# SyncE's first 40 transfers, each held until the third last has landed, in an attention and two-MoE kernel

## The chip, the cores and the metric

The kernel runs on one core of one Trainium2 chip. The metric is the time of one execution in microseconds of the device. Three runs of the kernel before gave a median of 592.82 us (592.39 to 595.15).

## What is computed

A gated linear attention with a state is followed by two expert-free feed-forward layers, all in 32-bit floats. The reference, cut to what matters:

```python
# attention: x [4, 8, 768, 32], a [4, 8, 768], B and C [4, 8, 768, 16], in chunks of 32
log_a = np.log(np.clip(a, 1e-06, 1.0))
for c in range(nc):
    L = np.exp(cum[:, :, :, None] - cum[:, :, None, :]) * causal      # cum: running sum of log_a
    y = (einsum('bhin,bhjn->bhij', C, B) * L) @ x                     # inside the chunk
    y += einsum('bhin,bhnd->bhid', C, state) * np.exp(cum)[..., None] # from the chunks before
    state = decay_full * state + sum_j(B_j x_j * decay_from_j)
# layer 1, tokens 3072 x 256:   h = x @ w_in (256 x 2048); x = (h * sigmoid(h)) @ w_out (2048 x 256)
# layer 2:                      h = x @ w_in
#   x = ((a0 + a1 h + a2 h^2 + a3 h^3) / (1 + |b0| |h| + |b1| h^2 + 1e-6)) @ w_out
```

## The kernel before

The 3072 tokens are 24 tiles of 128 tokens, tile `n` holding 128 positions of one of the 4 batches. For each of them one `tok` tile of 128 x 768 floats (384 KB: x, B and C in two layouts) is loaded (`attention`, line 668), into a ring of six. A visit of TensorE (`visit`, line 851) then makes that tile's attention, in one PSUM tile `att`, and the result is written as `y1h` and `y1l`, a rounded part and the rest, which the matmuls use in place of one 32-bit operand. Before a visit, VectorE or GpSimd multiply parts of the tile by decay factors: `Ea` at lines 720 and 724, `eL` at line 713. For the first three tiles the factors in `Ea` are computed in place. For all others they are computed once in two pieces, stored to the DRAM tensor `dre` (line 576) and loaded again, each row 16 times, by seven `Ea` loads (line 688, `E_LOADS`).

Layer 1 (`layer1_block`, line 954) goes through the tokens in six blocks of 512, and in each through 16 pieces of the hidden width: six matmuls of 128 x 512 into `h`, Silu, a split into two parts, six matmuls into `acc`. Its weights come in 16 raw tiles of 512 KB (`weights`, line 584, load in line 590, a ring of three `wraw` tiles), as 64-bit words that ScalarE, VectorE and GpSimd turn into two 32-bit parts `w` (lines 603 to 631). The weights of layer 2 take the same way, go out to DRAM as `w2s` and come back when layer 1 is done with its own. Layer 2 (`layer2_block`, line 1008) does the same with a rational function in place of Silu, and stores six output blocks.

All 113 transfers are issued by one engine, SyncE, in one order, and it stops at the first whose wait is not over. Which order this is, on SyncE and on every other engine, is decided when the program is built: each piece of work has a key (the table `K`, lines 34 and following), and a planner (`Plan.run`, line 243) starts, engine by engine, the ready piece with the smallest key, with its own costs per piece. The semaphores that the instructions wait for are then derived from the tiles that they share. Eight of them, DMAHW0 to DMAHW7, are used for transfers in turn; so a transfer already waits for the one eight places ahead of it.

The first transfers in order: `la` (the gates), `cum` and `con` (constants), four `tok` tiles, three `wraw` tiles, `abt` (the six coefficients), the two stores to `dre`, two `tok` tiles, and then `Ea` loads, `tok` tiles and `wraw` tiles mixed. Until the attention has begun, TensorE also runs 23 matmuls on zeros (line 530).

Of the kernel before, what the change touches and what calls it, by code (L numbers as in the profile page):

```python
# [7 lines left out]
F32 = mybir.dt.float32  # L8
# [6 lines left out]
P = 128  # L15
B, H, S, D, N = 4, 8, 768, 32, 16
# [8 lines left out]
WC = 2 * DM  # L25
# [4 lines left out]
NB2 = 512  # L30
HALVED = 0
HEAD = 0
TAIL_FLEX = 1
K = dict(
    half0=193.588,
# [150 lines left out]
R6 = NSUB + NCH  # L186
# [41 lines left out]
class Plan:  # L228
# [9 lines left out]
    def add(self, choices, key, deps=(), new=(), use=(), wr=(), rd=(), cols=0, after=0.0, big=True, soft=False):  # L238
        op = Op(choices, key, list(deps), list(new), list(use), wr, rd, cols, after, big, soft)
        self.ops.append(op)  # L240
        return op
# [94 lines left out]
def ssd_moe_moe_kernel(ctx: ExitStack, tc: tile.TileContext, tok, la_in, consts, w1, w2, ab, outT):  # L336
# [17 lines left out]
    def ring(tag, n, cols, dt=F32, space="SB", pad=0):  # L354
        rings[tag] = (Ring(n), n, cols, space, pad)

    counter = [0]

    def new(tag, dt=F32, cols=None):
        r, n, width, space, pad = rings[tag]  # L360
# [29 lines left out]
    def load_table(set_id):  # L390
        ACT.add_instruction(
            mybir.InstLoadActFuncSet(
                name=nc.get_next_instruction_name(),
                act_func_set_id=set_id,
                engine=mybir.EngineType.Activation,
                ins=[],
                outs=[],
            )
        )
# [60 lines left out]


    cum = new("cum")
    ld_la = add({"SP": (0.1, lambda: (load_table(SET_LN_EXP), nc.sync.dma_start(la, la_in)))}, 0.0)

    def f_cum():
        cum.t = cum.make()
        nc.sync.dma_start(cum.t[:, 0 : C_CEND - C_CUM], consts[:, C_CUM:C_CEND])

    ld_cum = dma(0.1, 197e3, f_cum, new=[cum])
    ld_con = dma(0.2, 101e3, lambda: nc.sync.dma_start(con, consts[:, 0:C_CUM]))  # L470
    ld_ab = dma(25.0, 3e3, lambda: nc.sync.dma_start(abt, ab))

    def f_ab():
        ACT.activation(absb, abt[:, 4:6], AF.Abs)
# [96 lines left out]
    for i, first in enumerate((0, NTB - P // H)):  # L571
        Ee, a = factors(lambda first=first: la[:, first * H : first * H + P], K["bulk"] + 2 * i, [], None)

        def f_dre(i=i, Ee=Ee, skip=0 if i == 0 else 2 * P // H - NTB):
            ns = slice(i * P // H, min(NTB, (i + 1) * P // H))
            nc.sync.dma_start(dre.rearrange("h n e -> n h e")[ns], Ee.t[skip * H :, 0 : P + R6])

        o_dre.append(dma(K["bulk"] + 2 * i, 68e3, f_dre, [a], use=[Ee]))
    decays(4, NTB, K["late"], [])
# [4 lines left out]
    def weights(layer, f, k_load, key):  # L584
        src = (w1, w2)[layer][f]
        raw = new("wraw", U64 if wide else F32)

        def f_load():
            raw.t = raw.make()
            nc.sync.dma_start(raw.t if wide else raw.t[:, 0:WC], src)  # L590

        o = dma(k_load, P * WC * (8 if wide else 4), f_load, new=[raw])
        val, value = raw, lambda: raw.t[:, 0:WC]
        if wide:
            v = new("wv")

            def words():
                w = raw.t.bitcast(U32).rearrange("p (n w) -> p n w", w=2)
                return w[:, :, 0], w[:, :, 1]

            def f_exp():
                v.t = v.make()
                ACT.activation(v.t, words()[1].bitcast(F32), AF.Prelu, scale=2.0**-112, alpha=2.0**32)  # L603

            def f_bits(part):
                low = words()[0]
                vb = v.t.bitcast(U32)
                if part == 0:
                    DVE.tensor_scalar(vb, vb, 3, None, op0=ALU.logical_shift_left)  # L609
                else:  # L610
                    DVE.scalar_tensor_tensor(vb, low, 29, vb, op0=ALU.logical_shift_right, op1=ALU.bitwise_or)  # L611

            o = add({"ACT": (c_act(WC) + 0.025, f_exp)}, key, [o], new=[v], use=[raw])
            for part in range(2):
                o = add({"DVE": (c_dve(WC, part == 0), lambda part=part: f_bits(part), True)}, key + 0.1, [o], use=[raw, v])
            val, value = v, lambda: v.t

        part = raw if layer else new(f"w{f}")

        def halves():  # L620
            t = part.t.bitcast(F32R)
            return t[:, WC : 2 * WC], t[:, 0:WC]

        def f_hi():
            if not layer:
                part.t = part.make()
            ACT.activation(halves()[0], value(), AF.Copy)

        def f_lo(eng):
            hi, lo = halves()  # L630
            eng.tensor_tensor(lo, value(), hi, op=ALU.subtract)  # L631

        a = add({"ACT": (c_act(WC), f_hi)}, key + 0.2, [o], new=[] if layer else [part], use=[val, part])
        o = add(
            {"POOL": (c_ptt(WC), lambda: f_lo(POOL), True), "DVE": (c_dve(WC), lambda: f_lo(DVE), True)},
            key + 0.3, [a], use=[val, part],
        )
        if layer:
            dr = new("w2s")

            def f_out():
                dr.t = dr.make()
                nc.sync.dma_start(dr.t, part.t.bitcast(F32))

            return dr, dma(key + 0.4, P * WC * 8, f_out, [o], new=[dr], use=[part])
        w_at[f], o_w[f] = part, o

    def reload(f, key, dr, after):
        part = new(f"w{f}")

        def f_in():
            part.t = part.make()
            nc.sync.dma_start(part.t, dr.t)

        w_at[f], o_w[f] = part, dma(key, P * WC * 8, f_in, [after], new=[part], use=[dr])

# [11 lines left out]
    def attention(n, T, d, k_load):  # L668
        b, c = blk_of[n], n % TPB
        o = n * P  # L670
        t = new("tok")

        def f_load():
            t.t = t.make()
            nc.sync.dma_start(t.t[:, 0:TOK], tok[n])  # L675

        ld = dma(k_load, P * TOK * 4, f_load, new=[t])
        x = lambda: t.t[:, 0:DM]
        bw = lambda: t.t[:, DM : DM + P]
        bt = lambda: t.t[:, DM + P : DM + 2 * P]  # L680
        cx = lambda: t.t[:, DM + 2 * P : TOK]
        cs = lambda: t.t[:, TOK : TOK + DM]

        for n0, n1 in E_LOADS:
            if n == n0:

                def f_er(n0=n0, n1=n1):
                    nc.sync.dma_start(Ev[:, n0:n1, :], dre[:, n0:n1, :].unsqueeze(1).broadcast_to([H, N, n1 - n0, P + R6]))

                first, end = n0 * H // P, (n1 - 1) * H // P  # L690
                o = dma(k_load, 155e3 * (n1 - n0), f_er, o_dre[first : end + 1])
                o_ee.update(dict.fromkeys(range(n0, n1), o))
        e0 = lambda: Ev[:, n, P : P + R6]

        Gm = new("Gm")

        def f_gm(eng):
            Gm.t = Gm.make()
            eng.tensor_tensor(
                Gm.t.rearrange("p (h a i) -> p h a i", h=H, a=SPC),  # L700
                eG[:, :, n * H : (n + 1) * H].rearrange("p a h -> p h a").unsqueeze(3).broadcast_to([P, H, SPC, SUB]),
                tri.rearrange("p (a i) -> p a i", a=SPC).unsqueeze(1).broadcast_to([P, H, SPC, SUB]),
                op=ALU.mult,
            )

        by = {"POOL": (1.06, lambda: f_gm(POOL), True), "DVE": (c_dve(H * CH), lambda: f_gm(DVE), True)}
        if n < GM_POOL:
            del by["DVE"]
        o_gm = add(by, T, [o_eG[n], ld_con], new=[Gm])

        def f_bw():
            v = bw().rearrange("p (h n) -> p h n", h=H)
            POOL.tensor_tensor(v, v, eL[:, n, :].unsqueeze(2).broadcast_to([P, H, N]), op=ALU.mult)

        o_bw = add({"POOL": (0.4, f_bw, True)}, T + 0.5 * d, [ld, o_eL[n]], use=[t])


        def f_ce(eng):
            v = cx().rearrange("p (a i) -> p a i", a=2)
            eng.tensor_tensor(v, v, Ev[:, n, 0:P].unsqueeze(1).broadcast_to([P, 2, P]), op=ALU.mult)  # L720

        def f_cs(eng):
            v, o = (z.rearrange("p (a s i) -> p a s i", a=2, s=NSUB) for z in (cx(), cs()))
            eng.tensor_tensor(
                o, v, e0()[:, 0:NSUB].unsqueeze(1).unsqueeze(3).broadcast_to([P, 2, NSUB, SUB]), op=ALU.mult
            )

        o_ce = add({"POOL": (0.8, lambda: f_ce(POOL), True), "DVE": (c_dve(DM), lambda: f_ce(DVE), True)}, T + 0.5 * d, [ld, o_ee[n]], use=[t])
        o_cs = add({"POOL": (0.58, lambda: f_cs(POOL), True), "DVE": (c_dve(DM), lambda: f_cs(DVE), True)}, T + 2 * d, [o_ce], use=[t])

        at[n] = (t, T, d, ld, o_bw, [o_ce], o_cs, o_gm, Gm, x, bw, cs, bt, cx, e0)
# [276 lines left out]
    def layer2_block(b, t0, step, rh, rc, held_h, o_tab):  # L1008
# [85 lines left out]
        for d in range(2):  # L1094
# [7 lines left out]
                    DVE.tensor_copy(ov()[:, d, :], acc_t[d])  # L1102

            def f_store(d=d):
                nc.sync.dma_start(outT[:, d, lo_t:hi_t], ov()[:, d, :])

            choices = {"ACT": (c_act(NB2, True), lambda f_o=f_o: f_o(ACT)), "DVE": (c_dve(NB2), lambda f_o=f_o: f_o(DVE))}
            if final:
# [163 lines left out]
```

## Time and profile before

| | before |
|---|---|
| median of three runs | 592.82 us (592.39 to 595.15) |
| the profiled execution | 591.67 us |
| its span, first to last instruction | 589.8 us |
| TensorE busy | 577.5 us, 98% |
| VectorE, ScalarE, GpSimd busy | 434.7, 405.7, 301.5 us |
| mean granted TensorE clock | 0.994 |
| moved by DMA | 48.84 MB |

The span is what the profile covers; the 1.9 us around it belong to the execution but show no instruction. Busy shares are means over stages that differ: attention with layer 1 up to about 150 us, layer 1 alone, then layer 2 from about 300 us. An idle time of an engine is listed with what ended it (the releaser). A transfer's time to landing runs from its issue on SyncE to the last of its semaphore's counts.

### The profile page before, as it was taken

What the parts mean: (1) busy time and instruction counts of PE and PEld (TensorE: products, weight loads), DVE (VectorE), ACT (ScalarE), POOL (GpSimd) and SP (SyncE); (2) the same over time, 40 slices, a digit from 0 to 9 for tenths busy, and PEclk for the clock granted to TensorE, in tenths of its full rate; (3) what the DMA queues carried; (4) which work ended last, traced back from release to release, by engine and by line L of the source; (5) the groups of instructions that cost most, each with busy time, mean ns of one, the idle gap of its engine ahead of it and who ended that gap; (6) DMA issues with size and microseconds to landing.
All of it is one profiled execution on the core that took longest, in us unless ns stands there. A gap on an engine that the chain in (4) does not pass through costs nothing.

```text
span 589.8 us, 11914 instructions
## 1 busy us (share of the span) xinstructions
PE 577.5 (98%) x4589; PEld 463.8 (79%) x4589; DVE 434.7 (74%) x722; ACT 405.7 (69%) x728; POOL 301.5 (51%) x328
## 2 busy tenths in 40 slices
PE   7799999999999999999999999999999999999997
PEld 4477777777888888888888888888888888888885
DVE  4899999888522222222124999999999999999995
ACT  4466666456433544444446899989999999999994
POOL 4354416541112100100102788888888888888883
PEclk9799999999999999999999999999999999999999
DMA  7876566876300000000047500000000000000000
GB/s 249 260 238 229 199 198 241 293 234 221 144 1 0 1 0 1 1 1 0 1 138 230 203 1 1 37 1 1 36 1 2 37 1 0 36 2 2 36 2 36
DMA packets 16200, 48.84 MB, mean 83 GB/s; under 512 B 1872, under 2 KB 2960, under 8 KB 16144
## 3 DMA queue, kind: packets, MB, share of 16 engines
q1 hardware_dynamic: 16144, 48.09, 24.0%
q8 instruction: 36, 0.59, 0.4%
q14 instruction: 20, 0.16, 0.1%
HBM read 36.44 MB, written 11.64 MB: 82 GB/s over the span
## 4 chain that ended last, share of the span: by engine, by line
PE 87%; DVE 6%; DMA 3%; ACT 2%; SPq 1%; issue 1%; DVEq 0%; ACTq 0%
PE acc L402 42%; PE h L402 34%; PE b L402 8%; PE att L402 3%; DMA wraw<-in_w_dram 2%; DVE wv L611 1%; DVE w L631 1%; DVE wv L609 1%; DMA Ea<-dre 1%; DVE M L768 1%; ACT wv L603 1%; SPq L675 0%; DVE y1l L896 0%; ACT T L976 0%; DVE S L789 0%
## 5 line engine op out<-in xcount | busy, mean ns | idle before, releaser
L402 PE MATMUL h<-y1h,w 128*128 128x512 f32 x636 | 216.9, 391 | 0.4 <-ACT y1h L893 0.3
L402 PE MATMUL acc<-gh,w 128*128 128x512 f32 x768 | 207.1, 391 | 0.0
L402 PEld LDWEIGHTS acc<-gh,w 128*128 128x128 f32 x768 | 143.1, 188 | 30.6 <-ACT wraw L1100 0.3
L941 DVE TENSOR_TENSOR gl<-T,gh 128x512 fp32r<-128x512 f32 x85 | 59.7, 705 | 115.6 <-ACT gh L935 90.4
L402 PEld LDWEIGHTS h<-y1h,w 128*128 128x128 f32 x636 | 119.3, 188 | 26.9 <-ACT y1h L893 0.8
L941 POOL TENSOR_TENSOR gl<-g,gh 128x512 fp32r<-128x512 f32 x95 | 122.8, 1295 | 19.4 <-ACT gh L935 16.5
L402 PE MATMUL h<-y1l,w 128*128 128x512 f32 x318 | 123.9, 390 | 0.3 <-DVE y1l L896 0.3
L402 PE MATMUL acc<-gl,w 128*128 128x512 f32 x384 | 118.5, 389 | 0.0
L976 ACT ACTIVATE T<-h 128x512 f32<-128x512 f32 x96 | 57.1, 596 | 80.6 <-PE h L402 78.3
L937 POOL TENSOR_SCALAR gh<-T 128x512 fp32r<-128x512 f32 x21 | 14.1, 670 | 167.0 <-PE acc L402 122.9
L402 PEld LDWEIGHTS acc<-gl,w 128*128 128x128 f32 x384 | 72.1, 188 | 15.2
L1042 POOL TENSOR_SCALAR tok<-T,abt 128x512 f32<-128x512 f32 x96 | 74.3, 774 | 9.3 <-ACT T L1034 8.7
L1045 DVE SCALAR_TENSOR_TENSOR b<-T,absb,b 128x512 f32<-128x512 f32 x96 | 71.6, 751 | 2.6 <-ACT T L1034 1.7
L1063 DVE SCALAR_TENSOR_TENSOR g<-tok,abt,b 128x512 f32<-128x512 f32 x96 | 71.2, 743 | 0.9 <-ACT b L1057 0.3
L1054 ACT ACTIVATE b<-b,lnb 128x512 f32<-128x512 f32 x96 | 64.5, 673 | 8.4 <-DVE b L1045 8.0
L402 PEld LDWEIGHTS h<-y1l,w 128*128 128x128 f32 x318 | 59.7, 188 | 12.7 <-DVE y1l L896 0.6
L935 ACT ACTIVATE gh<-T 128x512 fp32r<-128x512 f32 x75 | 47.4, 632 | 26.1 <-PE acc L402 25.4
L1057 ACT ACTIVATE b<-b 128x512 f32<-128x512 f32 x96 | 57.4, 599 | 0.5
L1051 DVE SCALAR_TENSOR_TENSOR tok<-T,abt,h 128x512 f32<-128x512 f32 x63 | 46.8, 744 | 0.7
L402 PE MATMUL b<-y1h,w 128*128 128x512 f32 x132 | 45.8, 389 | 0.0
L1048 DVE TENSOR_TENSOR h<-tok,h 128x512 f32<-128x512 f32 x63 | 43.4, 689 | 0.1
L1038 ACT ACTIVATE b<-h,abt 128x512 f32<-128x512 f32 x63 | 42.3, 672 | 0.2 <-DVE tok L1051 0.2
(68 smaller groups left out, 619.1 us busy)
## 6 DMA issues: line engine op xcount, KB each, us to landing
wraw<-in_w_dram SPq DMA_DIRECT2D x32, 512.0 KB, 4.5
tok<-in_tok_dram SPq DMA_DIRECT2D x24, 384.0 KB, 4.5
w2s<-wraw SPq DMA_DIRECT2D x16, 512.0 KB, 3.6
w<-w2s SPq DMA_DIRECT2D x16, 512.0 KB, 4.8
out_dram<-wraw SPq DMA_DIRECT2D x12, 256.0 KB, 2.1
Ea<-dre SPq DMA_DIRECT2D x3, 268.0 KB
Ea<-dre SPq DMA_DIRECT2D x2, 201.0 KB
cum<-in_consts_dram SPq DMA_DIRECT2D x1, 192.0 KB, 2.4
```

Of the source, the lines that this page charges most:

```text
L402: PE.matmul(out, lhsT, rhs, start=start, stop=stop)
L935: ACT.activation(gh.t[:, 0:W], g.t[:, 0:W], AF.Copy)
L941: eng.tensor_tensor(gl.t[:, 0:W], g.t[:, 0:W], gh.t[:, 0:W], op=ALU.subtract)
L976: ACT.activation(T.t[:, 0:w], h.t[:, 0:w], AF.Silu)
L1038: ACT.activation(c.t[:, 0:W], h.t[:, 0:W], AF.Abs, scale=abt[:, 4:5])
L1042: POOL.tensor_scalar(t1.t[:, 0:W], s.t[:, 0:W], abt[:, 3:4], abt[:, 1:2], op0=ALU.mult, op1=ALU.add)
L1045: DVE.scalar_tensor_tensor(c.t[:, 0:W], s.t[:, 0:W], absb[:, 1:2], c.t[:, 0:W], op0=ALU.mult, op1=ALU.add)
L1048: DVE.tensor_tensor(h.t[:, 0:W], t1.t[:, 0:W], h.t[:, 0:W], op=ALU.mult)
L1051: DVE.scalar_tensor_tensor(t1.t[:, 0:W], s.t[:, 0:W], abt[:, 2:3], h.t[:, 0:W], op0=ALU.mult, op1=ALU.add)
L1054: ACT.activation(c.t[:, 0:W], c.t[:, 0:W], AF.Ln, bias=lnb)
L1057: ACT.activation(c.t[:, 0:W], c.t[:, 0:W], AF.Exp, scale=-1.0)
L1063: DVE.scalar_tensor_tensor(g.t[:, 0:W], t1.t[:, 0:W], abt[:, 0:1], c.t[:, 0:W], op0=ALU.add, op1=ALU.mult)
```

## The change

A helper `move` takes the place of every `nc.sync.dma_start` of the kernel, eleven places in all. It issues the same transfer, and for those that are 4th to 40th in SyncE's order it adds a dependency on the one issued three places before: the transfer isn't issued until that one has landed. Which transfers there are, their order and their size stay.

```diff
+AHEAD, PACED = 3, 40
+PACE = mybir.DependencyInfo(mybir.DependencyClass.Sync, mybir.DependencyReason.DATA)
...
-    counter = [0]
+    counter, moves = [0], []
+
+    def move(out, src):
+        i = nc.sync.dma_start(out, src).ins
+        if AHEAD <= len(moves) < PACED:
+            tc.add_manual_dep(i, moves[-AHEAD], PACE, reason="pace")
+        moves.append(i.name)
...
-            nc.sync.dma_start(raw.t if wide else raw.t[:, 0:WC], src)
+            move(raw.t if wide else raw.t[:, 0:WC], src)
```

The other places are changed in the same way: the loads of `la`, `cum`, `con`, `abt`, `tok` and `Ea`, the stores to `dre`, `w2s` and the output, and the load of `w` from `w2s`.

On the other engines the order stays as it was. On SyncE the order stays too, and the waits differ. These are its rows from the second `tok` tile to the first `Ea` load, before (the names behind `waits` are semaphores, one for each of eight transfers in turn, or an engine's):

```order
L675 DMA tok_106<-in_tok_dram 128x768
L675 DMA tok_112<-in_tok_dram 128x768
L675 DMA tok_124<-in_tok_dram 128x768
L590 DMA wraw_138<-in_w_dram 128x512
L590 DMA wraw_152<-in_w_dram 128x512 [waits DMAHW0_49]
L590 DMA wraw_175<-in_w_dram 128x512 [waits DMAHW1_49]
L471 DMA abt<-in_ab_dram 128x6 [waits DMAHW2_49]
L576 DMA dre<-T_191 16x8x134 [waits DMAHW3_49,Activation_49]
L576 DMA dre<-T_197 8x8x134 [waits DMAHW4_49,Activation_49]
L675 DMA tok_210<-in_tok_dram 128x768 [waits DMAHW5_49]
L675 DMA tok_231<-in_tok_dram 128x768 [waits DMAHW6_49]
L688 DMA Ea<-dre 128x1x134 [waits DMAHW7_49,DMAHW3_49]
```

And with the change:

```order
L362 DMA tok_106<-in_tok_dram 128x768 [waits DMAHW1_49]
L362 DMA tok_112<-in_tok_dram 128x768 [waits DMAHW2_49]
L362 DMA tok_124<-in_tok_dram 128x768 [waits DMAHW3_49]
L362 DMA wraw_138<-in_w_dram 128x512 [waits DMAHW4_49]
L362 DMA wraw_152<-in_w_dram 128x512 [waits DMAHW5_49]
L362 DMA wraw_175<-in_w_dram 128x512 [waits DMAHW6_49]
L362 DMA abt<-in_ab_dram 128x6 [waits DMAHW7_49]
L362 DMA dre<-T_191 16x8x134 [waits DMAHW0_49,Activation_49]
L362 DMA dre<-T_197 8x8x134 [waits DMAHW1_49,Activation_49]
L362 DMA tok_210<-in_tok_dram 128x768 [waits DMAHW2_49]
L362 DMA tok_231<-in_tok_dram 128x768 [waits DMAHW3_49]
L362 DMA Ea<-dre 128x1x134 [waits DMAHW4_49]
```

The first four rows had no wait and now have one; each semaphore is the one of the transfer three places ahead (`la`, the first of all, counts on DMAHW0, `cum` on DMAHW1). The `Ea` load in the last row, for which only the first store to `dre` had to have landed, waits for the second (DMAHW4).

## Rows read from the trace of the kernel before

**Rows 1.** The page: TensorE's busy time (first), the chain that ended last (by engine).

```profile
PE 577.5 (98%) x4589; PEld 463.8 (79%) x4589; DVE 434.7 (74%) x722; ACT 405.7 (69%) x728; POOL 301.5 (51%) x328
...
PE 87%; DVE 6%; DMA 3%; ACT 2%; SPq 1%; issue 1%; DVEq 0%; ACTq 0%
```

**Rows 2.** Windows: stretch, busy us of each engine, TensorE's granted clock, DMA share, GB/s.

```profile
29.00:100.00 71.00, 69.14 (x1122) 53.03 (x1130) 66.59 (x132) 47.28 (x86) 33.40 (x31) 1.00 0.67 225
...
300.00:590.00 290.00, 286.09 (x1261) 236.08 (x1259) 263.51 (x400) 254.21 (x458) 224.92 (x239) 1.00 0.11 38
```

**Rows 3.** Timeline, TensorE: start, duration, instruction, idle before it and releaser.

```profile
28.32 0.50 PE L402 MATMUL h<-y1h,w 128*128 128x512 f32 x1 [0.28 <-ACT y1h L893]
```

**Rows 4.** Timeline, SyncE's queue: start and length of issue, number of transfers.

```profile
2.12 1.85 SPq L675 DMA_DIRECT2D tok<-in_tok_dram x4
...
6.13 0.47 SPq L471 DMA_DIRECT2D abt<-in_ab_dram x1
11.83 1.80 SPq L576 DMA_DIRECT2D dre<-T x2
...
14.65 1.28 SPq L688 DMA_DIRECT2D Ea<-dre x2
...
26.21 1.10 SPq L675 DMA_DIRECT2D tok<-in_tok_dram x2
...
54.94 4.72 SPq L675 DMA_DIRECT2D tok<-in_tok_dram x2
```

**Rows 5.** By line: tok at 2.12, 3.55, 14.13, 18.07, 19.77, 26.98, 37.20; wraw 5.64, 42-50.

```profile
DMA to landing us min/median/max: 4.5/4.5/4.5
...
DMA to landing us min/median/max: 6.1/6.1/6.1
...
DMA to landing us min/median/max: 4.2/4.2/4.2
...
DMA to landing us min/median/max: 7.8/7.8/7.8
...
DMA to landing us min/median/max: 9.7/9.7/9.7
...
DMA to landing us min/median/max: 5.4/5.4/5.4
...
DMA to landing us min/median/max: 2.9/2.9/2.9
...
DMA to landing us min/median/max: 7.7/7.7/7.7
...
DMA to landing us min/median/max: 3.6/4.1/4.7
```

**Rows 6.** Timeline, VectorE.

```profile
2.70 0.26 DVE L478 TENSOR_SCALAR la<-la 128x192 f32<-128x192 f32 x1 [2.70 <-DMA la<-in_la_dram]
...
18.64 0.43 DVE L720 TENSOR_TENSOR tok<-tok,Ea 128x256 f32<-128x256 f32 x1 [0.91 <-DMA Ea<-dre]
...
30.99 1.55 DVE L720 TENSOR_TENSOR tok<-tok,Ea 128x256 f32<-128x256 f32 x3
```

**Rows 7.** The page's DMA issues: number, KB each, median us to landing.

```profile
cum<-in_consts_dram SPq DMA_DIRECT2D x1, 192.0 KB, 2.4
...
dre<-T SPq DMA_DIRECT2D x1, 67.0 KB, 2.5
```

**Rows 8.** Windows, as in rows 2, of the start.

```profile
2.70:9.53 6.83, 6.83 (x52) 4.70 (x51) 2.60 (x7) 2.05 (x8) 2.66 (x4) 1.00 0.97 322
9.53:16.35 6.82, 2.92 (x60) 1.69 (x58) 5.53 (x11) 3.13 (x8) 5.20 (x7) 1.00 0.70 240
16.35:23.18 6.83, 6.33 (x167) 3.33 (x168) 4.62 (x11) 3.29 (x7) 1.55 (x4) 0.50 1.00 285
```

**Rows 9.** The chain that ended last, in order of time: start, duration, what.

```profile
4.93 7.23 DMA wraw<-in_w_dram
...
14.65 3.89 DMA Ea<-dre
```

More of the change, by code (lines that the diff above doesn't have):

```diff
@@ L462, in ssd_moe_moe_kernel @@
     cum = new("cum")
-    ld_la = add({"SP": (0.1, lambda: (load_table(SET_LN_EXP), nc.sync.dma_start(la, la_in)))}, 0.0)
+    ld_la = add({"SP": (0.1, lambda: (load_table(SET_LN_EXP), move(la, la_in)))}, 0.0)
     def f_cum():
         cum.t = cum.make()
-        nc.sync.dma_start(cum.t[:, 0 : C_CEND - C_CUM], consts[:, C_CUM:C_CEND])
+        move(cum.t[:, 0 : C_CEND - C_CUM], consts[:, C_CUM:C_CEND])
     ld_cum = dma(0.1, 197e3, f_cum, new=[cum])
-    ld_con = dma(0.2, 101e3, lambda: nc.sync.dma_start(con, consts[:, 0:C_CUM]))
-    ld_ab = dma(25.0, 3e3, lambda: nc.sync.dma_start(abt, ab))
+    ld_con = dma(0.2, 101e3, lambda: move(con, consts[:, 0:C_CUM]))
+    ld_ab = dma(25.0, 3e3, lambda: move(abt, ab))
     def f_ab():
@@ L575, in f_dre @@
             ns = slice(i * P // H, min(NTB, (i + 1) * P // H))
-            nc.sync.dma_start(dre.rearrange("h n e -> n h e")[ns], Ee.t[skip * H :, 0 : P + R6])
+            move(dre.rearrange("h n e -> n h e")[ns], Ee.t[skip * H :, 0 : P + R6])
         o_dre.append(dma(K["bulk"] + 2 * i, 68e3, f_dre, [a], use=[Ee]))
@@ L642, in f_out @@
                 dr.t = dr.make()
-                nc.sync.dma_start(dr.t, part.t.bitcast(F32))
+                move(dr.t, part.t.bitcast(F32))
             return dr, dma(key + 0.4, P * WC * 8, f_out, [o], new=[dr], use=[part])
@@ L652, in f_in @@
             part.t = part.make()
-            nc.sync.dma_start(part.t, dr.t)
+            move(part.t, dr.t)
         w_at[f], o_w[f] = part, dma(key, P * WC * 8, f_in, [after], new=[part], use=[dr])
@@ L674, in f_load @@
             t.t = t.make()
-            nc.sync.dma_start(t.t[:, 0:TOK], tok[n])
+            move(t.t[:, 0:TOK], tok[n])
         ld = dma(k_load, P * TOK * 4, f_load, new=[t])
@@ L687, in f_er @@
                 def f_er(n0=n0, n1=n1):
-                    nc.sync.dma_start(Ev[:, n0:n1, :], dre[:, n0:n1, :].unsqueeze(1).broadcast_to([H, N, n1 - n0, P + R6]))
+                    move(Ev[:, n0:n1, :], dre[:, n0:n1, :].unsqueeze(1).broadcast_to([H, N, n1 - n0, P + R6]))
                 first, end = n0 * H // P, (n1 - 1) * H // P
@@ L1104, in f_store @@
             def f_store(d=d):
-                nc.sync.dma_start(outT[:, d, lo_t:hi_t], ov()[:, d, :])
+                move(outT[:, d, lo_t:hi_t], ov()[:, d, :])
             choices = {"ACT": (c_act(NB2, True), lambda f_o=f_o: f_o(ACT)), "DVE": (c_dve(NB2), lambda f_o=f_o: f_o(DVE))}
```

## Prediction

> Transfers are counted in the order in which SyncE issues them: 1 is the load of `la`, 4 to 7 are the first four `tok` tiles, 8 to 10 the first three raw weight tiles, 12 and 13 the two stores to `dre`, 16 the `Ea` load for token tile 3. The change holds 37 of them, 4 to 40.
>
> **What bounds the kernel now.** I read the page first: TensorE is busy in 98% of the span and carries 87% of the chain that ended last, DMA 3% [rows 1]. Then the windows, to see where TensorE has any air. From 29 to 100 us it is idle for 1.9 of 71 us, and from 300 to the end for 3.9 of 290 us [rows 2]; between them the chain runs through it without a rest. All the rest of its idle time lies before 29 us, and so do most of the transfers that the change holds: number 31 goes out at 37.2 us. So the question is by how much the first layer-1 matmul, at 28.32 us [rows 3], and the attention visits that follow it come later. What is lost there can't be won back: behind it TensorE rests for under 6 us up to the end, and that rest follows its own supply, which would move along.
>
> Next I read SyncE's own queue. Number 11 is out by 6.6 us; then it stands until 11.83 us at the first `dre` store, and later until 26.21 us at a `tok` load [rows 4]. Last, the time from issue to landing: a `tok` load takes 4.5 us as the first of its row, 4.2 us at 14.1 us and 9.7 us at 19.8 us, where nothing else is in its way 2.9 us; the third weight tile takes 7.7 us [rows 5]. The difference, 1.3 to 6.8 us, is time that a transfer spends behind others. That is the cover under which a later issue costs nothing.
>
> **The change, part by part.** No instruction is moved and no byte is added or taken. SyncE computes nothing, so the extra waits themselves cost nothing. What counts is who stands behind each wait.
>
> *The first row, transfers 4 to 11.* `la` has landed at 2.70 us, when VectorE starts on it [rows 6]. So the first `tok` is issued at about 2.75 us and not at 2.12 us: 0.6 us late. The next two wait for `cum` (1.19 + 2.4 = 3.6 us [rows 7]) and `con`. The fourth, number 7, waits until number 4 has landed, at 2.12 + 4.5 + 0.6 = 7.2 us. That sounds bad, but in the trace of before it was issued at 3.55 us and landed 6.1 us later [rows 5], at 9.6 us, and 7.2 + 2.9 = 10.1 us is again 0.5 to 0.6 us late. The same sum holds for 8, 9 and 10. The DMA engines were 97% busy from 2.70 to 9.53 us, at 322 GB/s [rows 8], so no later piece can gain much either. Cost: **+0.6 us**. Ends: if number 4 takes 2.9 us as a lone one does, it lands at 5.65 us, 1.0 us early; if the second and third hold bite as well, +1.0 us. I take the plain shift, since the full engines are nearest to the row.
>
> *The `dre` stores and the `Ea` load behind them, 12 to 16.* Today 12 is let go by ScalarE's exponentials at 11.83 us. Now it also waits for number 9, which landed at 12.16 us [rows 9] and would at 12.8 us. Number 13, issued at 12.6 us today, waits for 10 (5.64 + 7.7 = 13.4, now 14.0 us). The pair of stores takes 1.80 us to issue [rows 4], some 1.1 us of it the second, so the two `tok` loads go out at 15.1 and 15.5 us, 1.4 us late. Number 16 was issued at 14.65 us as soon as 12 had landed; now it waits for 13 too, 14.0 + 2.5 [rows 7] = 16.5 us. It landed 3.89 us after its issue [rows 9], just behind number 15 (14.13 + 4.2 = 18.3 us). With 15 at 15.5 + 4.2 = 19.7 us it lands near 20.0 us where it was 18.54 us: 1.5 us late, of which 0.6 us are already counted. VectorE stands still for exactly this landing, 0.91 us before L720 [rows 6], so nothing hides it. Cost: **+0.9 us**. Ends: 0, if the number of transfers ahead and not the issue sets the landing; +1.4 us, if the whole 2.0 us of later issue shows.
>
> *Transfers 17 to 30.* Here the issues move by 3 to 8 us, since each `Ea` load is slow and the third last is often one. The cover is widest here as well: number 23 took 9.7 us. The narrowest place I find is number 25, the `tok` tile issued at 26.21 us. It will wait for 22, which lands between 20 (18.07 + 7.8 = 25.9 us [rows 5]) and 23 (29.5 us); I take 28 us, with the shift 29.5 to 30.5 us. Then 25 lands at 32.4 us (2.9 us alone) to 34.7 us (4.2 us). VectorE wants it for the third of the L720 that begin at 30.99 us [rows 6], so at about 32.0 us, now 33.5 us. That is −1.1 to +1.2 us, and a stop can't be negative. Cost: **+0.7 us**; ends 0 and +3 (the first rival).
>
> *Transfers 31 to 40.* They are issued between 37.2 us and 55 us [rows 4, 5], ten in 18 us, and the weight tiles among them land 3.6 to 4.7 us after their issue where they are thickest [rows 5]. Three of them need 5.3 us on average to be issued, so the third last has landed. Cost: **0**.
>
> The sum is +2.2 us. The profiled execution took 591.67 us, of which 589.8 us are span; with the sum 593.9 us. The median of the three runs, 592.82 us, lies 1.15 us above the profiled one, so on its scale I forecast **595.0 us**, 0.37% more. About 0.5%, or 3.0 us, is what a measurement of this kernel can tell from no change.
>
> **The rivals.**
> *A, three are too few: slower.* From 14 to 26 stand 13 transfers; the last of them lands at 26.98 + 5.4 = 32.4 us [rows 5], and with the shift may do so at 33.9 us. The first goes out at 15.1 us, so there are 18.8 us. With three in flight one lands every third of the time L from issue to landing; 13 L/3 passes 18.8 us where L is over 4.3 us. That is the point from which this rival decides. For L = 5.0 us the stretch takes 21.7 us, 2.9 us more: 595.0 + 2.9 = 597.9 us. For it: 4.5 us for number 4, 5.4 us for number 26, and six of the 13 are `Ea` loads, one of which took 3.89 us. Against: those times hold queueing behind more than two others. Chance 0.27. The Trainium skill, DMA: Bandwidth & Descriptors, Rules for kernel authors, says to issue a transfer early and to wait late, so that its fixed setup overlaps; that speaks against this change. Its section on the anatomy of one DMA puts the fixed part at about 2.0 us for transfers issued by GpSimd; nine groups of three from 4 to 30 would by that estimate cost 18 us, 610.8 us in all. The trace agrees only that there is a fixed part (2.9 us for a lone `tok`), and the 4.2 to 9.7 us of the others show that most of it is covered.
>
> *B, TensorE's clock: slower.* TensorE was busy for 2.92 us of the stretch from 9.53 to 16.35 us, and in the next one, to 23.18 us, the granted clock was 0.50, that is 1.2 GHz, the lower of its two levels [rows 8]. The attention visits in that stretch would start about 1 us later. If the clock stays low for one more stretch of 6.83 us, work that fills it takes up to 3.4 us more: 598.4 us. For it: longer rests. Against: at 6.33 us of 6.83 us the engine was fully occupied, and would still be for over 5. Chance 0.08.
>
> *C, a shorter row lands sooner: faster.* If each held transfer takes what a lone one does, number 4 gains 1.0 us and 15 another 1.3 us, and the later ones up to that much again: −1.0 to −3.5 us, 591.8 to 589.3 us. For it: 2.9 us against 4.2 to 9.7 us. Against: a transfer's queueing is behind others that go first anyway, in an order that stays. Chance 0.12, 0.07 of it beyond 3.0 us.
>
> *D, the cover is whole, or the waits hold nothing:* 592.8 us. For it: SyncE already waited, by its eight semaphores in turn, for the eighth last. Against: VectorE stands for number 16. Chance 0.11.
>
> **How the numbers follow.** My forecast, +0.7 to +2.9 us, has 0.42. Same: 0.42 + 0.11 + 0.05 of C = 0.58. Slower by over 0.5%: A and B, 0.35. Faster: 0.07. The range for 8 in 10 goes from 592.0 us (most of D in it, C out) to 598.5 us (A up to L = 5.2 us): it leaves out C's 0.12 and the far end of A. The likeliest sign is slightly slower, within what a measurement can tell.
>
> **What would show it.** In the profile after, L720 at 18.64 us should start near 20.1 us, the first layer-1 matmul at 28.32 us near 30, and from 40 us on all of TensorE's work about 2 us later, with the same idle time up to the end. Time from issue to landing should fall to 3 to 4.2 us before 30 us. Wrong, if TensorE stops anew for a weight or a `tok` between 30 and 60 us (A), if the clock row is 0.50 behind 23.2 us (B), or if L720 starts before 18.6 us (C).

## The result: slower by 0.73%, and the profile after

The kernel with the change takes 597.11 us in the median of 13 runs (594.57 to 600.31), the kernel before 592.6 us (591.27 to 595.15); the ratio is 1.0073, with a 95% interval from 1.0054 to 1.0093, so +4.3 us (3.2 to 5.5). That is past the 3.0 us that a measurement of this kernel can tell. The forecast was 595.0 us, with a change of less than 0.5% as the likeliest case. The time lies inside the range, and on the side of rival A, whose worked example gave 597.9 us.

The profiled execution took 597.42 us (span 595.5 us), 5.75 us more than the one before; that is 1.4 us more than the ratio says, mostly since before lay 0.9 us below its median and after 0.3 us above. The lines of the page that answer to [rows 1]:

```profile
PE 579.9 (97%) x4585; PEld 464.8 (78%) x4589; DVE 434.9 (73%) x722; ACT 407.4 (68%) x728; POOL 299.3 (50%) x328
...
PE 86%; DMA 8%; DVE 5%; issue 1%; ACT 0%; SPq 0%; DVEq 0%
```

TensorE's share of the chain has hardly moved, DMA's went from 3% to 8%. Where that is, the chain in order of time shows, from 1.2 to 44 us (start, duration, what; the pieces of 0.02 to 0.05 us between them left out):

```profile
1.20 2.78 DMA cum<-in_consts_dram
...
3.99 4.01 DMA tok<-in_tok_dram
...
8.02 4.91 DMA wraw<-in_w_dram
...
12.94 4.17 DMA abt<-in_ab_dram
...
17.12 0.35 SPq L362
...
17.52 4.15 DMA tok<-in_tok_dram
...
21.73 0.33 SPq L362
...
22.10 5.80 DMA Ea<-dre
...
27.92 5.78 DMA Ea<-dre
...
33.77 3.56 DMA tok<-in_tok_dram
...
37.40 5.40 DMA wraw<-in_w_dram
...
42.85 0.56 issue
43.41 0.37 ACT y1h L901
```

This is rival A drawn by the profile: a transfer lands, the third one behind it is issued 0.02 us later, lands, and so on, with nothing but SyncE's issuing between them from 1.20 to 42.81 us. In the kernel before, the same stretch held two DMA pieces [rows 9] and otherwise SyncE's issuing, VectorE, ScalarE and TensorE. The eight links from 3.99 us on make up 37.8 us, so 4.7 us each; rival A decides where a transfer takes over 4.3 us.

The same in the engines. First SyncE's queue (start, length of issue, number of transfers), for [rows 4]:

```profile
2.81 3.88 SPq L362 DMA_DIRECT2D tok<-in_tok_dram  x4
...
14.54 1.89 SPq L362 DMA_DIRECT2D dre<-T  x2
17.12 0.82 SPq L362 DMA_DIRECT2D tok<-in_tok_dram  x2
17.99 2.85 SPq L362 DMA_DIRECT2D Ea<-dre  x2
...
33.77 1.74 SPq L362 DMA_DIRECT2D tok<-in_tok_dram  x2
```

Then VectorE (idle time before and its releaser in brackets; L728 is the L720 of before, eight lines lower) and TensorE's first layer-1 matmul, for [rows 6] and [rows 3]:

```profile
21.66 0.43 DVE L728 TENSOR_TENSOR tok<-tok,Ea 128x256 f32<-128x256 f32 x1 [1.92 <-DMA tok<-in_tok_dram]
...
36.35 0.76 DVE L728 TENSOR_TENSOR tok<-tok,Ea 128x256 f32<-128x256 f32 x2 [2.04 <-DMA Ea<-dre]
37.35 0.42 DVE L728 TENSOR_TENSOR tok<-tok,Ea 128x256 f32<-128x256 f32 x1 [0.25 <-DMA tok<-in_tok_dram]
```

The first bracket names a `tok` load, number 15, which landed at 21.67 us. Tile 3 doesn't use it. What its L728 still lacked was number 16, the `Ea` load: the last count of that semaphore came at 21.57 us, so VectorE stood for the same landing as before, 3.0 us later.

```profile
31.03 0.49 PE L410 MATMUL h<-y1h,w 128*128 128x512 f32 x1 [0.28 <-ACT y1h L901]
```

The first layer-1 matmul is 2.7 us late, and then TensorE stops anew. Windows of after (columns as in [rows 2]):

```profile
5.00:10.00 5.00, 4.75 (x45) 3.36 (x46) 2.20 (x5) 1.38 (x6) 2.71 (x4) 1.00 0.93 293
30.00:35.00 5.00, 3.75 (x30) 2.51 (x16) 4.23 (x10) 2.46 (x5) 2.45 (x3) 1.00 0.66 179
40.00:45.00 5.00, 3.68 (x46) 2.34 (x44) 4.73 (x10) 2.50 (x5) 0.80 (x1) 1.00 0.77 260
...
300.00:590.00 290.00, 290.00 (x1279) 239.61 (x1278) 264.88 (x402) 256.61 (x462) 225.59 (x239) 1.00 0.11 39
```

And of before:

```profile
5.00:10.00 5.00, 5.00 (x46) 3.33 (x46) 2.31 (x5) 1.38 (x6) 3.13 (x5) 1.00 1.00 369
30.00:35.00 5.00, 5.00 (x24) 4.13 (x23) 4.93 (x11) 3.97 (x7) 4.35 (x6) 1.00 0.96 342
40.00:45.00 5.00, 5.00 (x112) 4.03 (x113) 4.51 (x12) 3.10 (x6) 3.50 (x3) 1.00 0.78 238
```

There TensorE was busy for all 5.00 us of both 30 to 35 and 40 to 45 us. Behind 50 us the shift stays at about 5.5 us up to the end, and no rest swallows any of it. The granted clock is 1.00 in each of these rows, so rival B has no part in it. In the other executions of the change the mean granted clock was 0.98 to 0.99 in all but one, at 594.6 to 600.3 us; the two at 1.00 took 596.2 and 597.4 us. So a lower clock doesn't make the 4.3 us there either.

### The profile page after: what moved, and what is told of

It is laid out like the page before. It is cut to its first block, busy times and chain, and to the rows that moved or that the text cites. A ratio compares the mean times of both kernels' runs of the same rounds, so it can differ in the third digit from the quotient of the medians.

```text
span 595.5 us, 11906 instructions
## 1 busy us (share of the span) xinstructions
PE 579.9 (97%) x4585; PEld 464.8 (78%) x4589; DVE 434.9 (73%) x722; ACT 407.4 (68%) x728; POOL 299.3 (50%) x328
## 3 DMA queue, kind: packets, MB, share of 16 engines
HBM read 36.44 MB, written 11.64 MB: 81 GB/s over the span
## 4 chain that ended last, share of the span: by engine, by line
PE 86%; DMA 8%; DVE 5%; issue 1%; ACT 0%; SPq 0%; DVEq 0%
PE acc L410 42%; PE h L410 33%; PE b L410 8%; PE att L410 3%; DMA wraw<-in_w_dram 3%; DMA tok<-in_tok_dram 2%; DMA Ea<-dre 2%; DVE wv L619 1%; DMA abt<-in_ab_dram 1%; DVE w L639 1%; DVE wv L617 1%; DVE M L776 1%; DMA cum<-in_consts_dram 0%; DVE tok L732 0%; DVE S L797 0%
```

## Experiments

The ratio is to the kernel before, with its 95% interval; "+1.2 us" is the ratio less 1, times 592.7 us. Line numbers and the numbers of transfers are as above.

### Which part of the 37 held transfers costs it

Four kernels hold one piece each, a fifth all but the last piece. The only edit is to the condition in `move`; in hold_4_11 and hold_4_30 it is made by setting `PACED` to 11 and 30, which comes to the lines written out here:

```diff
-        if AHEAD <= len(moves) < PACED:
+        if AHEAD <= len(moves) < 11:       # hold_4_11
+        if 11 <= len(moves) < 16:          # hold_12_16
+        if 16 <= len(moves) < 30:          # hold_17_30
+        if 30 <= len(moves) < 40:          # hold_31_40
+        if AHEAD <= len(moves) < 30:       # hold_4_30
```

> Only transfers 4 to 11 are held. Theory (a chain from landing to issue: with three in flight each transfer takes 3.5 to 5.8 us from issue to landing, and it costs as long as it lasts): number 10 lands about 2.3 us later, as it did with the whole change, then eight in flight catch up; the first layer-1 matmul 0.5 to 1.5 us later than 28.32 us and the time +0.5 to +1.5 us, 593 to 594. Rival 1 (the late first row is all of it): first layer-1 matmul near 31.0 us, +4 to +5 us, 596.5 to 597.5. Rival 2 (only the handover at dre and Ea, 12 to 16): within 0.5 us of 592.6.

Measured: 1.0021 (1.0005 to 1.0036), +1.2 us. The third weight tile, number 10, was issued at 10.4 us and took 6.2 us, so it landed at 16.6 us, later than with the whole change (15.7 us) and 3.2 us later than before. L728 for tile 3 began at 20.49 us, 1.85 us late, and the first layer-1 matmul at 29.66 us, 1.3 us late. So of 3.2 us about a third reached the end. Rival 1 falls. Rival 2 falls by the two rows; by the time alone it would not, since the interval begins at +0.3 us.

> Only transfers 12 to 16 are held. Theory (a chain over all of 4 to 30): one piece of it, L728 for tile 3 at 19.3 to 20.0 us where it was 18.64 us, and +0.7 to +1.4 us, 593.3 to 594. Rival 1 (the first row): within 0.5 us of 592.6. Rival 2 (the handover at dre and Ea is all of it): L728 near 21.7 us and +4 to +5 us, 596.5 to 597.5.

Measured: 1.0009 (0.9996 to 1.0021), +0.5 us. L728 began at 19.39 us, 0.75 us late, as the theory had it; the time is a little under the theory's +0.7 to +1.4 us. Rival 2, that this handover is all of it, falls; a cost of nothing isn't excluded.

> Only transfers 17 to 30 are held; up to 18.6 us all is as before. Theory (chain): seven of them are Ea loads that take 5 to 6 us each with three in flight, so this is the largest piece: first layer-1 matmul unmoved to 0.5 us late, attention visits from 35 us on 3 to 4 us late, +2.5 to +4 us, 595 to 596.5. Rivals 1 and 2 (first row or handover alone): within 0.7 us of 592.6.

Measured: 1.0022 (1.0004 to 1.0040), +1.3 us; the theory's 2.5 to 4 us were too much. (Of the seven `Ea` loads six lie in this piece; number 16 doesn't.) The first layer-1 matmul came at 27.84 us, 0.5 us earlier than before, so half a microsecond between two profiles carries no weight. The attention visit that began at 39.90 us before began at 40.46 us, 0.6 us late, and the one of 53.26 us 1.8 us late, where 3 to 4 us were expected. TensorE's added idle time lies behind it: it was busy for 4.54 us of the 5 us from 40 us on, and for 47.2 us of 50 to 100 us, where it was 48.3 us before. The interval begins at +0.2 us, so by the time alone this piece could also cost next to nothing.

> Only transfers 31 to 40 are held. All theories: ten transfers in 18 us are less than three in flight deliver, so within 0.5 us of 592.6. If it costs 1 us or more, the weight tiles from 36 us on are part of the chain too.

Measured: 0.9985 (0.9970 to 0.9999), −0.9 us. Nothing had forecast a gain, so it was run again:

> The kernel of hold_31_40 once more, since it measured 0.15% under the kernel before (0.9985, 0.9970 to 0.9999), which no theory had expected. If a shorter row is worth something where three in flight deliver enough: again 0.997 to 0.9995. If it was chance: 0.9995 to 1.002.

Measured: 0.9994 (0.9977 to 1.0010). By the numbers that I had named, 0.9994 lies on the side of a gain, by 0.0001; its interval holds 1. So a gain isn't shown, and neither is that the first result was chance. Holding 31 to 40 costs nothing that can be seen.

> Transfers 4 to 30 are held, 31 to 40 are free. Theory (one unbroken chain: a held piece by itself is partly caught up by the eight in flight behind it, which the next held piece prevents): as the whole change, +3.7 to +5.2 us, 596.4 to 597.9. Rival (the pieces add up, each for itself: 1.0 + 0.6 + 1.3 us): +2.3 to +3.3 us, 595 to 596.

Measured: 1.0071 (1.0049 to 1.0092), +4.2 us: the whole cost of the change, without 31 to 40. The pieces by themselves make 1.2 + 0.5 + 1.3 = 3.0 us. That is below 4.2 us, as one unbroken chain would have it, but the interval of +4.2 us begins at 2.9 us. Whether the pieces more than add up stays open.

### How many in flight are enough

```diff
-AHEAD, PACED = 3, 40
+AHEAD, PACED = 4, 40       # ahead_4; 2 and 6 in the others
```

> Transfers 5 to 40 wait for the fourth last. Theory (time to landing grows more slowly than the number in flight, because each transfer has a start-up that others cover): 4.7 us with three in flight, near 5.2 us with four, so one lands every 1.3 us where the kernel before needs 1.2 us: number 30 lands 1 to 3 us late (8.5 us late with three) and the time is +0.5 to +2 us, 593.1 to 594.6. Rival (only the handover from dre to Ea, where with four the Ea load 16 waits for no more than before): within 0.5 us of 592.6.

Measured: 1.0010 (0.9990 to 1.0031), +0.6 us. This can't tell the theory from the rival.

> Transfers 3 to 40 wait for the second last. Theory: time to landing between the 2.9 us of a lone tok load and the 4.7 us with three in flight, near 3.8 us, so one lands every 1.9 us where the kernel before needs 1.2; number 30 lands about 18 us late and the time is +8 to +15 us, 600.5 to 607.5. Rival (a handover or two): +5 to +7 us, below 600.

Measured: 1.0288 (1.0252 to 1.0324), +17.1 us; more than the theory's +8 to +15, and far from the rival's 5 to 7. The chain of this kernel:

```profile
1.19 2.40 DMA cum<-in_consts_dram
3.61 3.16 DMA tok<-in_tok_dram
6.78 3.54 DMA tok<-in_tok_dram
10.34 4.43 DMA wraw<-in_w_dram
14.78 4.17 DMA wraw<-in_w_dram
...
19.04 2.15 DMA dre<-T
21.21 3.97 DMA tok<-in_tok_dram
25.19 2.28 DMA Ea<-dre
```

One transfer of two is no faster by half: a `tok` takes 3.2 to 4.0 us where three in flight give 3.6 to 4.2 us in the chain above, a weight tile 4.2 to 4.4 us where they give 4.9 to 5.4 us.

> Transfers 7 to 40 wait for the sixth last, so the added waits are there and hold little. Theory: six in flight land faster than one every 1.2 us, so within 0.7 us of 592.6. Rival (the wait instructions themselves cost): +1 us or more.

Measured: 1.0000 (0.9980 to 1.0020). The waits are there and cost nothing that can be seen (−1.2 to +1.2 us), so the instructions that carry them aren't the 4.3 us.

The four kernels make a table. Number 4's issue and number 26's are from SyncE's queue, and 26 lands by its own time (5.4, 4.9, 3.7 and 4.5 us). The fourth column is the time from number 4's issue to number 26's landing, divided by the 23 transfers; the last is that time multiplied by the number held in flight: how long one occupies its place.

| in flight | 4 issued | 26 landed | for each of 23 | place occupied |
|---|---|---|---|---|
| eight (before) | 2.12 us | 32.4 us | 1.32 us | not held |
| four | 2.12 us | 32.7 us | 1.33 us | up to 5.3 us |
| three (the change) | 2.81 us | 38.9 us | 1.57 us | 4.7 us |
| two | 3.61 us | 48.3 us | 1.94 us | 3.9 us |

The program asks for one transfer every 1.32 us (the expectations above say 1.2 us). Four in flight deliver that (and may have places free, so that 5.3 us is an upper bound), three don't. Halving the number from four to two takes at most about a quarter from the time that each needs.

### The dre stores' own wait

The row of before shows the first `dre` store let go at 11.83 us by ScalarE, which ran two exponentials behind a weight tile's conversion. This kernel swaps them on ScalarE's order alone, once in the kernel before and once with the change:

```diff
-    for op in plan.run():
+    ops = plan.run()
+    first = next(op for op in ops if op.choices[op.eng][1].__name__ == "f_exp")
+    ops.remove(first)
+    ops.insert(max(ops.index(o.deps[0]) for o in o_dre) + 1, first)
+    for op in ops:
```

> The kernel before, with one move on ScalarE alone: the two exponentials whose results go to dre stand before the first weight tile's conversion (L603) and no longer behind it. In the kernel before that conversion waits for a weight tile to land (10.96 us), TensorE has their input ready by 9.85 us, and the first dre store goes out at 11.83 us. Theory (VectorE's 0.91 us stop at L720 for the Ea load 16 is the end of a chain through that store, so a version without the conversion in it is faster): the store goes out at 10.2 to 10.6 us, L720 for tile 3 starts 0.5 to 0.9 us earlier, and the time is -0.4 to -0.9 us, 591.7 to 592.2. Rival (the full DMA engines or the conversion, now later, set the end): within 0.3 us of 592.6, or up to 0.5 us more.

Measured: 0.9989 (0.9971 to 1.0008), so no gain that can be told. The store went out at 10.83 us, 1.0 us earlier, number 16 no longer stops VectorE, and still L720 came only 0.12 us earlier. The first weight tile's conversion, ScalarE's L603 and VectorE's L609, before:

```profile
10.96 0.68 ACT L603 ACTIVATE wv<-wraw 128x512 f32<-128x512 f32 x1 [3.12 <-DMA wraw<-in_w_dram]
...
11.67 1.03 DVE L609 TENSOR_SCALAR wv<-wv 128x512 uint32<-128x512 uint32 x1 [0.95 <-ACT wv L603]
```

And in this kernel, followed by VectorE up to L720:

```profile
11.64 0.68 ACT L603 ACTIVATE wv<-wraw 128x512 f32<-128x512 f32 x1 [0.40 <-DMA wraw<-in_w_dram]
...
12.36 1.22 DVE L609 TENSOR_SCALAR wv<-wv 128x512 uint32<-128x512 uint32 x1 [0.77 <-ACT wv L603]
...
17.58 0.42 DVE L609 TENSOR_SCALAR wv<-wv 128x512 uint32<-128x512 uint32 x1
17.91 0.69 DVE L699 TENSOR_TENSOR Gm<-eG,con 128x512 f32<-128x512 f32 x1
18.52 0.62 DVE L720 TENSOR_TENSOR tok<-tok,Ea 128x256 f32<-128x256 f32 x1
```

There is no bracket at L720 any more: the 0.91 us of waiting have become VectorE's own work, which begins 0.7 us later because the conversion that feeds it does. The exponentials in front are not what delays that conversion: ScalarE was done with them and stood for 0.40 us more, until the weight tile landed. That tile came at 11.64 us in this profile and at 10.69 to 11.38 us in the five others that leave transfers 4 to 11 free. So what the earlier store would be worth with the tile in its usual place isn't shown by these rows; the time shows no gain.

> The same move on ScalarE, in the changed kernel with 4 to 40 held at three in flight. Theory (in the changed kernel the issue of the dre stores hangs on landings, of transfers 9 and 10, and not on the exponentials): the move is worth nothing, 597.1 within 0.8 us, and the first store goes out at 14.5 us as before the move. Rival (the stores still hang on ScalarE): 0.5 to 1 us less than 597.1 and the store out before 14.2 us.

Measured: 1.0066 (1.0043 to 1.0089), 596.85 us against 597.11 us: no gain that can be told, as the theory said. The two intervals are too wide to exclude the rival's 0.5 us; the rows decide. ScalarE and SyncE:

```profile
9.13 0.51 ACT L560 ACTIVATE T<-h 128x134 f32<-128x134 f32 x2 [2.38 <-PE h L410]
```

```profile
13.93 1.89 SPq L362 DMA_DIRECT2D dre<-T  x2
```

The exponentials are done by 9.64 us and the store goes out 4.3 us later, so it hangs on a landing. It left 0.6 us earlier than in the profile of after, which falls under the number that I had named for the rival; ScalarE's part in it is excluded by the 4.3 us all the same.

### Is it a delay, or work of the DMA engines?

Each `tok` and weight tile among the first 40 in two transfers of 64 partitions, both held until both pieces of the third last tile have landed:

```diff
+    def move(out, src, cut=False):
+        names = []
+        for h in (slice(0, P // 2), slice(P // 2, P)) if cut and len(moves) < PACED else (slice(0, None),):
+            i = nc.sync.dma_start(out[h], src[h]).ins
+            if AHEAD <= len(moves) < PACED:
+                for name in moves[-AHEAD]:
+                    tc.add_manual_dep(i, name, PACE, reason="pace")
+            names.append(i.name)
+        moves.append(names)
```

Not shown: the two calls that load `tok` and weight tiles pass `True` for `cut`.

> The changed kernel, with each tok and weight tile among the first 40 loaded in two transfers of 64 partitions, one behind the other; both wait for both pieces of the third last tile. So the bytes in flight stay what three whole transfers are, and the number of transfers in flight for these tiles is six. Theory (the fixed part of a time to landing, some 2.3 us by 3.8 us with two and 4.5 us with three in flight, is a delay in which a tile holds its place, so the rate follows from the bytes in flight): as the whole change, number 30's counterpart lands at 44 to 48 us, 596.3 to 598.5. Rival 1 (a start takes time of the DMA engines, which two starts for a tile double): 599 or more. Rival 2 (the number of transfers decides, as with six whole ones in flight): 595 or less.

Measured: 1.0221 (1.0198 to 1.0245), 605.64 us, +13.1 us, 8.8 us more than whole tiles at the same bytes in flight. The theory falls. Windows of this kernel:

```profile
5.00:10.00 5.00, 4.30 (x43) 2.91 (x44) 1.85 (x5) 1.38 (x6) 1.85 (x3) 1.00 0.98 260
5.00:50.00 45.00, 34.35 (x670) 21.64 (x671) 29.40 (x62) 18.03 (x38) 16.45 (x21) 1.00 0.80 207
```

The kernel with two in flight (ahead_2), for comparison:

```profile
5.00:10.00 5.00, 4.21 (x42) 2.82 (x43) 1.75 (x5) 1.38 (x6) 1.70 (x2) 1.00 0.76 225
```

From 5 to 10 us the DMA engines are busy for 0.98 of the time and move 260 GB/s; in after 0.93 and 293 GB/s, in the kernel before 1.00 and 369 GB/s (both above). Divided by the share, a fully busy second carries 265, 315 and 369 GB, with two held 296. So with the tiles cut, each byte takes more of the engines' busy time, and that far the run is on the side of rival 1. Rival 1's reason, a fixed time for each start, isn't shown, and the single packets of the trace speak against it: one of 4096 bytes takes 159 ns in the median with whole transfers, whether two, three or eight are in flight, and 256 ns here; one of 3072 bytes takes 121 and 161 ns (packets that start from 2 to 60 us). A time paid once for each start would lengthen a few packets of a transfer and leave the median where it was. Why most packets of a cut tile take longer stays open. Nor is it all of the 8.8 us: SyncE's issuing is 9.2% of this kernel's chain up to 60 us, 5.5 us, where the change with whole tiles has 1.2 us. How the 8.8 us divide between the two isn't separated. The Trainium skill, DMA: Bandwidth & Descriptors, Rules for kernel authors, advises against two transfers to disjoint halves of the partitions, since both use the same engines. This run agrees: 605.64 against 597.11 us.

## Why the prediction was right in its range and wrong in its sum

**The likeliest case failed, rival A came.** The time lies in the range because the range had been carried up to rival A with L = 5.2 us, and not because the sum was right: its +2.2 us came to +4.3 us. A change of less than 0.5% had a chance of 0.58, rival A 0.27. What bounds the kernel was right: what is lost before TensorE runs without a rest is not won back, and the shift that TensorE has at 50 us still stands at the end. That D (no cost) has gone is shown by the interval, that C (faster) has gone by L728 at 21.66 us, B by the clock rows.

**The first row, +0.6 us.** Number 4 did not come 0.6 us late but landed at 2.81 + 3.5 = 6.3 us, earlier than the 6.65 us of before; inside the ends. But the same shift was carried over to 8, 9 and 10 ("The same sum holds"), and there it failed: number 10 landed at 10.3 + 5.4 = 15.7 us, 2.3 us late, beyond the end of +1.0; held by itself this row cost +1.2 us of the time. The reason that I gave, DMA engines 97% busy [rows 8], was a state that eight in flight make. With three, the engines are less busy and get less done while busy: 0.93 and 293 GB/s where it was 1.00 and 369.

**The stores and the Ea load, +0.9 us.** Right in size. L728 began at 21.66 us and not near 20.1, but these 1.6 us are the first row's error handed on (number 10 at 15.7 in place of 14.0 us). L728 is 3.0 us late in all; less the first row's 2.3 us that leaves 0.7 us for this term, and it measures +0.5 us by itself (a cost of nothing isn't excluded).

**Transfers 17 to 30, +0.7 us.** This is the other term that was sized too small and kept the forecast too low. It rests on times to landing of "3 to 4.2 us before 30 us"; the lines of after for the two `tok` loads and for the weight tile issued from 21.7 to 29 us are

```profile
DMA to landing us min/median/max: 4.0/5.1/6.3
...
DMA to landing us min/median/max: 5.1/5.1/5.1
```

and the `Ea` loads in the chain take 5.8 us. A lone `tok`'s 2.9 us and the 4.2 us of a short queue were the wrong rows to size it by; the 5.0 us that served rival A as an example was the better one. With it the 13 transfers from 14 to 26 were to take 21.7 us, and they took 38.9 − 17.1 = 21.8 us. I took number 25 for the narrowest place; VectorE stopped 2.04 us for an `Ea` load and 0.25 us for 25. From L728's 3.0 us the shift grows to 5.7 us of span: 2.7 us for this term in place of 0.7, within its end of +3. That is by one pair of profiles, which lie 5.75 us apart where the medians lie 4.5 us apart; held by itself, the piece cost +1.3 us (0.2 to 2.4).

**Transfers 31 to 40, 0.** Right: measured twice, and once more by leaving them free in hold_4_30, which costs as much as the whole.

**The chances.** The threshold of rival A, 4.3 us for a place, was right, and the rows spoke for being past it: 4.5 us for number 4, 5.4 us for 26. I discounted them as queueing behind more than two others. The table shows that this discount is small: from three to two in flight a place is occupied for 4.7 and 3.9 us, not for two thirds. The Trainium skill, DMA: Bandwidth & Descriptors, Rules for kernel authors, which would have a transfer issued early and waited for late, spoke against the change, and the runs agree in sign. The 18 us that the prediction estimated from the Trainium skill's fixed part (DMA: Bandwidth & Descriptors, the anatomy of one DMA) are far from the measured 4.3 us. Three in flight still cover most of what a lone transfer waits for.

None of the versions tried is shown to be faster than the kernel before: `exps_first` at 0.9989 has 1 inside its interval, and so has the second of the two measurements of `hold_31_40` (0.9985, then 0.9994).

## What to carry to other kernels

Before transfers are held back, count them where they are thickest, take the time for each that the program asks for (here 1.32 us) and multiply it by the number that may be in flight: if that is less than the time that one occupies its place (3.96 against 4.7 us here), the hold becomes the chain. Size that place by transfers of the crowded stretch, since it shrinks much less than the number in flight does. And a row that shows the DMA engines full holds for the queue depth at which it was taken, and no longer when the change lowers it.

## What the runs showed of the hardware

- GB/s divided by the busy share of the DMA engines, from 5 to 10 us: 369 with up to eight transfers in flight, 315 with three, 296 with two, 265 with three tiles in two pieces each. The fall with whole transfers shows in that stretch alone: from 15 to 40 us the quotient is 318 with up to eight, 326 with four, 300 with three, 308 with two, and 273 with the cut tiles.
- A packet of 4096 bytes takes 159 ns in the median with whole transfers at each depth, and 256 ns when the tile is loaded as two halves of 64 partitions.
- A low granted clock at the start did not make the first layer-1 matmul late. With six in flight the mean granted clock of the first 30 us was 0.72, in the kernel before 0.89, with the change 1.00:

```profile
0.00:30.00 30.00, 23.65 (x463) 12.82 (x464) 18.94 (x41) 12.13 (x27) 12.50 (x22) 0.72 0.81 244
```

The first layer-1 matmul of that kernel still came at 28.49 us (28.32 us before). That a low clock costs nothing in all isn't shown: of the 98 executions of the kernel before that were measured beside the experiments, the 22 with a mean granted clock of 0.990 or less took 594.0 us in the median, the 34 with 0.995 or more 592.3 us.
